# Attention, MoE and a second MoE layer on one core: every transpose of the attention on 128 rows, with an identity of exchanged halves

## The chip, the cores and the metric

The kernel runs on one core of a Trainium2 chip. The metric is the device time of one execution in microseconds (us). The engines are PE (TensorE: a matmul, and PEld, the load of its stationary operand), DVE (VectorE), ACT (ScalarE), POOL (GpSimd) and SP, which only issues transfers.

## What is computed

Two batches of twelve causal attention heads (448 positions, 64 wide) feed two feed-forward layers over 896 tokens. The reference, cut:

```python
scores = scale * np.matmul(q, k.transpose(0, 1, 3, 2))
scores = np.where(np.triu(np.ones((seq, seq), dtype=bool), k=1), -1e9, scores)
attn = np.exp(scores - scores.max(-1, keepdims=True))
x = np.matmul(attn / (attn.sum(-1, keepdims=True) + 1e-9), v)     # 2 x 12 heads
x = x.transpose(0, 2, 1, 3).reshape(896, 768)
x = ((1 / (1 + np.exp(-(x @ w_gate)))) * (x @ w_val)) @ w_out     # 768 -> 1536 -> 768
h = x @ w_in                                                      # 768 -> 1024
solu = h * softmax(h)
out = (solu - mean(solu)) / sqrt(var(solu) + 1e-6) * g_ln @ w_out2
```

## The kernel before, in words

Precision: each fp32 operand of a matmul is split into a high and a low part, and three of the four products are summed. The split of scores and values is done on POOL, ACT and DVE while the attention runs.

**Staging.** The attention (the first quarter of the time) is written as a software pipeline over `slots` = 96 steps: 24 heads with four blocks of queries each. In each step the order of each engine's work is written out by hand: first PE (`sc_mm`, the side step `rm`, the transposes `tr_mm`, a piece of `pv_mm`), then ACT, DVE, POOL. The table `SIDE` says in which step of a pair of heads (eight steps) each side task falls; `UNIT0` says it for the transposes. Then come the gate and value products (L594), the products with `w_out` (L621), the second layer's `h` (L651), its transposes (L694) and its output products (L712), all on PE.

**Blocks of queries.** The 448 queries of a head are cut as 64 + 128 + 128 + 128 (`QE`), but a block of scores always has 128 rows: in the first block the upper 64 rows are other data, and only rows 64 to 127 count. The keys are cut in 128s. So the block of the scores on the diagonal of key block j has its 64 useful rows in partitions 64 to 127; the queries of its partitions 0 to 63 come before these keys, and are masked.

**Transposes.** `tr_mm(h, u)` turns the exponentials `p` of head h, unit u, on PE: `p` is the stationary operand, a 128x128 identity `ident` the moving one, and the result goes to the PSUM tile `t`, which ACT (`tr_hi`) and DVE (`tr_lo`) split into `pt`. A full block takes 128 rows of `p` and moves 128 columns of `ident`. A half block takes partitions 64 to 127 alone and moves the 64x64 corner of `ident`. `sorted(blocks, ...)` puts the half blocks of a unit first. A unit with u = 1 has two half and three full blocks; one with u = 0 has one half and three full blocks for a head of even number, and two and three for an odd one (with the extra half block of the last keys, which `last_keys`, the step `lk`, has put there). `rs_mm(p)`, the step `rm`, does the same once for each pair of heads with the reciprocals of the sums, spread by POOL into `rx` (`rs_wide`, the step `rx`): one half block and three full ones.

**Names in the rows.** `s` is the scores' PSUM tile (4 buffers), `qks` the split queries and keys, `x` the values' product, `r` and `rb` the transposed reciprocals, `sum` and `rs` the sums and their reciprocals. L345 is `sc_mm`, L360 `sc_exp`, L354 `sc_max`, L383 `rs_mm`, L410 `tr_mm`, L417 `tr_hi`, L439 `pv_mm`, L241 the high part of q, L251 the low part of q, L365 `sums`, L369 `recips`, L446 `x_mul`. L230 is every subtraction and L220, L222, L224 every copy of the helpers, told apart by their tiles: POOL's L230 on `qks` is the low part of a key (`kl0`, `kl1`), POOL's L222 to `rx` is `rs_wide`, ACT's L220 to `qks` is the high part of the pair's second key (`kh1`), to which `kl1` must wait.

Of the kernel before, what the change touches and what calls it, by code (L numbers as in the profile page):

```python
# [10 lines left out]
F32 = mybir.dt.float32  # L11
# [8 lines left out]
B, H, S, D = 2, 12, 448, 64  # L20
# [4 lines left out]
QE = [64, 192, 320, 448]  # L25
POFF = [0, 128, 384, 768, 1280]
# [18 lines left out]
def attn_moe_moe2(ctx: ExitStack, tc: tile.TileContext, qk, v, w_gv, w_out, w_in2, w_out2, g_ln, out):  # L45
# [3 lines left out]
    nc = tc.nc  # L49
    ctx.enter_context(tc.manual_schedule())  # L50

    const = ctx.enter_context(tc.tile_pool(name="const", bufs=1))
# [4 lines left out]
    NGA = 1  # L57

    ident = const.tile([128, 128], F32, name="ident")
    identb = const.tile([128, 128], BF16, name="identb")  # L60
    maskb = const.tile([128, 128], BF16, name="maskb")
    g_sb = const.tile([128, NF2], F32, name="g_sb")
# [129 lines left out]
    with ExitStack() as actx:  # L192
# [89 lines left out]
        nc.vector.memset(warm, 0.0)  # L282
        nc.scalar.activation(out=warm, in_=warm, func=AF.Exp)
        make_identity(nc, ident)
        nc.vector.tensor_copy(out=identb, in_=ident)
        mask0 = one.tile([128, 128], F32, name="mask0")
        nc.gpsimd.memset(mask0, 0.0)
# [11 lines left out]
        p_t = [one.tile([128, POFF[NQ]], F32, name=f"p{i}") for i in range(NPB)]  # L299

        for i in range(NPB):
            for j in range(NQ - 1):
                nc.vector.memset(p_t[i][:, POFF[j] + QE[j]:POFF[j + 1]], 0.0)
        for i in range(2):
            for a in range(2):
                nc.scalar.copy(out=v2[i][:, a, :, D:2 * D], in_=zero.rearrange("p (j d) -> p j d", j=3))

        ps = ps_x.tile([128, S], F32, tag="x", name="warm")
# [69 lines left out]
        def rs_mm(p):  # L378
            ps = ps_rr[p] = ps_x.tile([128, S], F32, tag="x", name="r")
            rx = rx_t.pop(p).rearrange("p i a d -> p i (a d)")  # L380
            for i in range(NQ):
                lo = 0 if i else D
                nc.tensor.transpose(ps[:, QE[i] - 128 + lo:QE[i]], rx[lo:, i], ident[lo:, lo:])  # L383

        def rs_out(p):
            rb_t[p] = xfp.tile([128, S], F32, tag="rb", name="rb")
# [7 lines left out]
        def tr_width(h, u):  # L394
            return 512 if u or h % 2 else S

        def tr_mm(h, u):
            ps = ps_tr[h, u] = ps_t.tile([128, 512], F32, tag="t", name="t")
            pt = p_t[h % NPB]
            n, blocks = 0, []  # L400
            for j in UNITS[u]:
                for i in range(j, NQ):
                    lo = 64 if i == j else 0
                    blocks.append((lo, i, j, n))
                    n += 128 - lo
            if n < tr_width(h, u):
                blocks.append((64, 3, 3, n))

            for lo, i, j, n in sorted(blocks, key=lambda x: -x[0]):
                nc.tensor.transpose(ps[:, n:n + 128 - lo], pt[lo:, POFF[i] + j * 128:POFF[i] + (j + 1) * 128],  # L410
                                    ident[lo:, lo:])

        def tr_hi(h, u):
            if h not in pt_t:
# [45 lines left out]
        def early_tiles():  # L460
# [27 lines left out]
            vh=9, vl=11, xl=23, rr=12, lk=5)  # L488
        STEP = dict(
            sm=(sums, 'P'), rc=(recips, 'D'), rx=(rs_wide, ENG['rx']), rm=(rs_mm, 'E'), rr=(rs_out, ENG['rr']),  # L490
            xm=(x_mul, 'D'), xh=(x_hi, ENG['xh']), xl=(x_lo, ENG['xl']),
            vh=(prep_v_hi, ENG['vh']), vl=(prep_v_lo, ENG['vl']), lk=(last_keys, ENG['lk']),
# [27 lines left out]
        for s in range(slots + 32):  # L520
# [5 lines left out]
            if s >= 110 and left and next(early):  # L526
                left -= 1
            units(tr_mm, s)
            next(pv_now, None)

# [46 lines left out]
    with tc.tile_pool(name="psg", bufs=8, space=PSUM, reuse_waits="tile") as psg:  # L577
        for t in range(NF):
            bs = (1,) if t < NE else (0, 1)
            ps = {}  # L580
            ev = {}
            for i in range(2):
                c = 2 * t + i
# [23 lines left out]
    for m in range(NK):  # L607
        pm = php.tile([128, B, 512], F32, tag="h", name="pm")
        ps = [pm[:, b, :S] for b in range(B)]
        for i in range(2):  # L610
            c = 2 * NF + 2 * m + i
# [168 lines left out]
```

## Time and profile before

| | |
|---|---|
| time, median of 3 runs | 525.12 us (523.32 to 526.01) |
| profiled execution: its own time | 524.13 us |
| profiled execution: its span in the trace | 522.3 us |
| PE busy | 510.7 us, 98% of the span |
| DVE, POOL, ACT busy | 356.6 us (68%), 219.1 us (42%), 200.7 us (38%) |

The span runs from the first to the last recorded instruction; the own time of the same execution is 1.83 us longer. The shares are means over stages that differ: the attention occupies all four engines, the stages behind it mostly PE. The profile's PE time of one matmul includes its way through the array, so the spacing of two matmuls is read from their starts, not from their durations.

### The profile page before, as it was taken

What the parts mean: (1) busy time and instruction counts of PE and PEld (TensorE: products, weight loads), DVE (VectorE), ACT (ScalarE), POOL (GpSimd) and SP (SyncE); (2) the same over time, 40 slices, a digit from 0 to 9 for tenths busy, and PEclk for the clock granted to TensorE, in tenths of its full rate; (3) what the DMA queues carried; (4) which work ended last, traced back from release to release, by engine and by line L of the source; (5) the groups of instructions that cost most, each with busy time, mean ns of one, the idle gap of its engine ahead of it and who ended that gap; (6) DMA issues with size and microseconds to landing.
All of it is one profiled execution on the core that took longest, in us unless ns stands there. A gap on an engine that the chain in (4) does not pass through costs nothing. (4 is left out here: it accounts for less than half of the span.)

```text
span 522.3 us, 7577 instructions
## 1 busy us (share of the span) xinstructions
PE 510.7 (98%) x2786; PEld 458.1 (88%) x2786; DVE 356.6 (68%) x539; ACT 200.7 (38%) x446; POOL 219.1 (42%) x297
## 2 busy tenths in 40 slices
PE   6999999999999999999999999999999999999997
PEld 5888888888999998888988899999998888899997
DVE  5788888886566788778778766777782888741210
ACT  5678777784512323231332231212221434341211
POOL 4888999965313332322332331111142479720000
PEclk9999999999999999999999999999999999999999
DMA  7954645103333333443443333443431131000101
GB/s 200 286 141 118 155 111 137 49 20 118 125 122 90 125 110 111 149 162 127 155 131 122 130 122 100 162 153 132 158 122 60 61 122 62 0 31 30 61 31 60
DMA packets 15125, 58.30 MB, mean 112 GB/s; under 512 B 2160, under 2 KB 2672, under 8 KB 15088
## 3 DMA queue, kind: packets, MB, share of 16 engines
q1 hardware_dynamic: 15088, 57.81, 35.1%
q8 instruction: 22, 0.36, 0.3%
q14 instruction: 15, 0.12, 0.1%
HBM read 55.05 MB, written 2.75 MB: 111 GB/s over the span
## 5 line engine op out<-in xcount | busy, mean ns | idle before, releaser
L594 PE MATMUL gv<-xy,hl 128*128 128x448 f32 x828 | 170.5, 367 | 3.3 <-DVE hl L134 3.3
L594 PEld LDWEIGHTS gv<-xy,hl 128*128 128x128 f32 x828 | 154.5, 188 | 19.1 <-DVE hl L134 6.2
L621 PE MATMUL pm<-g,hl 128*128 128x448 f32 x432 | 87.7, 365 | 0.0
L621 PEld LDWEIGHTS pm<-g,hl 128*128 128x128 f32 x432 | 81.2, 188 | 6.4
L111 ACT ACTIVATE raw<-raw 128x768 f32<-128x768 f32 (+1 forms) x56 | 47.5, 858 | 56.4 <-DMA raw<-in_gv_dram 27.4
L114 DVE TENSOR_SCALAR t<-raw 128x768 int32<-128x768 int32 (+1 forms) x56 | 40.7, 726 | 34.8 <-ACT raw L111 33.5
L712 PE MATMUL po<-wo,lt 128*128 128x384 f32 x336 | 60.7, 340 | 0.0
L116 DVE SCALAR_TENSOR_TENSOR t<-raw,t 128x768 int32<-128x768 int32 (+1 forms) x56 | 59.4, 1060 | 1.9
L188 POOL TENSOR_TENSOR g<-wk,g 128x448 fp32r<-128x448 f32 x24 | 27.3, 1158 | 77.9 <-ACT g L187 77.9
L651 PE MATMUL h<-wi,xy 128*128 128x512 f32 x252 | 59.2, 395 | 0.0
L712 PEld LDWEIGHTS po<-wo,lt 128*128 128x128 f32 x336 | 58.7, 188 | 0.2 <-POOL wo L643 0.2
L651 PEld LDWEIGHTS h<-wi,xy 128*128 128x128 f32 x252 | 47.2, 187 | 11.4
L119 DVE SCALAR_TENSOR_TENSOR t<-raw,t 128x768 int32<-128x768 int32 (+1 forms) x56 | 53.5, 956 | 1.7
L130 POOL TENSOR_SCALAR hl<-t 128x768 fp32r<-128x768 f32 x36 | 34.3, 954 | 40.9 <-PE pm L621 29.9
L439 PE MATMUL x<-pt,v 128*128 128x448 f32 (+3 forms) x252 | 47.8, 323 | 0.0
L360 ACT ACTIVATE p<-s,sum 128x448 f32<-128x448 f32 (+1 forms) x96 | 46.2, 491 | 1.8 <-DVE sum L354 1.7
L345 PE MATMUL s<-qks 128*128 128x448 f32 (+1 forms) x192 | 43.8, 328 | 2.7 <-ACT p L360 1.6
L410 PE MATMUL t<-ident,p 128*128 128x128 f32 (+1 forms) x228 | 39.7, 284 | 0.0
L439 PEld LDWEIGHTS x<-pt,v 128*128 128x128 f32 x252 | 37.6, 190 | 0.7
L354 DVE TENSOR_REDUCE sum<-s 128x1 f32<-128x448 f32 (+1 forms) x96 | 36.7, 415 | 2.0 <-PE s L345 1.3
L134 DVE TENSOR_TENSOR hl<-t,hl 128x768 fp32r<-128x768 f32 x36 | 34.3, 952 | 3.8 <-POOL hl L130 3.7
L345 PEld LDWEIGHTS s<-qks 128*128 128x128 f32 x192 | 33.2, 209 | 3.9 <-POOL qks L230 2.1
(83 smaller groups left out, 539.8 us busy)
## 6 DMA issues: line engine op xcount, KB each, us to landing
raw<-in_gv_dram SPq DMA_DIRECT2D x24, 768.0 KB, 4.5
raw<-in_wo_dram SPq DMA_DIRECT2D x20, 768.0 KB, 4.3
qkr<-in_qk_dram SPq DMA_DIRECT2D x46, 224.0 KB, 3.9
raw<-in_wi_dram SPq DMA_DIRECT2D x12, 512.0 KB, 3.5
vr<-in_v_dram SPq DMA_DIRECT2D x12, 256.0 KB, 2.6
out_dram<-o SPq DMA_DIRECT2D x6, 384.0 KB, 2.3
qkr<-in_qk_dram SPq DMA_DIRECT2D x4, 112.0 KB, 2.6
out_dram<-o SPq DMA_DIRECT2D x2, 192.0 KB, 1.9
```

The costliest lines, as they stand in the source:

```text
L111: nc.scalar.activation(out=w1.bitcast(F32), in_=w1.bitcast(F32), func=AF.Copy, scale=2.0 ** -112)
L114: nc.vector.tensor_scalar(out=tt, in0=w1, scalar1=3, scalar2=None, op0=ALU.logical_shift_left)
L116: nc.vector.scalar_tensor_tensor(out=tt, in0=w1, scalar=-2 ** 31, in1=tt, op0=ALU.bitwise_and, op1=ALU.bitwise_or)
L119: nc.vector.scalar_tensor_tensor(out=tt, in0=w0, scalar=29, in1=tt, op0=ALU.logical_shift_right, op1=ALU.bitwise_or)
L345: nc.tensor.matmul(out=o, lhsT=l, rhs=r, start=(m == 0), stop=(m == 2))
L360: nc.scalar.activation(out=p_t[h % NPB][:, POFF[i]:POFF[i] + n], in_=ps_sc.pop(s), func=AF.Exp, bias=mx, scale=1.0, accum_out=sm)
L410: nc.tensor.transpose(ps[:, n:n + 128 - lo], pt[lo:, POFF[i] + j * 128:POFF[i] + (j + 1) * 128], ident[lo:, lo:])
L439: nc.tensor.matmul(out=ps[:, 128 * j:], lhsT=l, rhs=pt_t[h][:, c, u, c0:c0 + S - 128 * j], start=(n == 0), stop=(n == 20))
L594: nc.tensor.matmul(out=ps[i, b], lhsT=w[:, a, cs], rhs=xy[kk][:, x, b * S:(b + 1) * S], start=(kk == 0 and a == 0 and x == 0), stop=(kk == ...
L621: nc.tensor.matmul(out=ps[b], lhsT=w[:, a, cs], rhs=g_t[kk][:, x, b * S:(b + 1) * S], start=(kk == 0 and a == 0 and x == 0), stop=(kk == N ...
L651: nc.tensor.matmul(out=h[:, n * 512:(n + 1) * 512], lhsT=xy[kk][:, a, tk], rhs=wi[n * NK + kk][:, c], start=(kk == 0 and i == 0), stop=(kk ...
L712: nc.tensor.matmul(out=ps[n], lhsT=lts[k // 4][:, a, k % 4], rhs=wo[k][:, c, cs], start=(k == 0 and i == 0), stop=(k == NF2 - 1 and i == 2))
```

## The change

A second identity `identx` is made, whose column halves are exchanged. Every half block now takes all 128 rows of `p` (or `rx`) and moves 128 columns: its transposed 64 useful rows land where they did, and the transposed other 64 rows land beside them, in 64 columns of the same PSUM tile that a full block of the same unit writes afterwards. Where the half block stands at the start of its tile (or of the tile's first 64 columns), there are no columns to its left, so the useful half is turned to the left by `identx` and the other half lies to its right. The last 64 columns of `p` are set to zero once at the start, since the extra half block of a head of odd number now reads its other 64 rows there. The number and order of PE's transposes stay as they are: 228 in `tr_mm` and 48 in `rs_mm`, 84 and 12 of them half blocks. POOL has two copies more at the start, DVE three memsets.

```diff
@@ -57,6 +57,7 @@
     ident = const.tile([128, 128], F32, name="ident")
+    identx = const.tile([128, 128], F32, name="identx")
...
@@ -282,6 +283,9 @@
         make_identity(nc, ident)
+
+        nc.gpsimd.tensor_copy(out=identx[:, :D], in_=ident[:, D:])
+        nc.gpsimd.tensor_copy(out=identx[:, D:], in_=ident[:, :D])
         nc.vector.tensor_copy(out=identb, in_=ident)
...
@@ -301,6 +305,7 @@
             for j in range(NQ - 1):
                 nc.vector.memset(p_t[i][:, POFF[j] + QE[j]:POFF[j + 1]], 0.0)
+            nc.vector.memset(p_t[i][:, POFF[3] + QE[3]:], 0.0)
...
@@ -379,8 +384,8 @@
             for i in range(NQ):
-                lo = 0 if i else D
-                nc.tensor.transpose(ps[:, QE[i] - 128 + lo:QE[i]], rx[lo:, i], ident[lo:, lo:])
+
+                nc.tensor.transpose(ps[:, max(QE[i] - 128, 0):max(QE[i], 128)], rx[:, i], ident if i else identx)
...
@@ -407,8 +412,9 @@
             for lo, i, j, n in sorted(blocks, key=lambda x: -x[0]):
-                nc.tensor.transpose(ps[:, n:n + 128 - lo], pt[lo:, POFF[i] + j * 128:POFF[i] + (j + 1) * 128],
-                                    ident[lo:, lo:])
+                c = max(n - lo, 0)
+                nc.tensor.transpose(ps[:, c:c + 128], pt[:, POFF[i] + j * 128:POFF[i] + (j + 1) * 128],
+                                    identx if lo > n else ident)
```

## Rows read from the trace of the kernel before

**Rows 1.** Page, engines: busy us, share of the span, instructions.

```profile
PE 510.7 (98%) x2786; PEld 458.1 (88%) x2786; DVE 356.6 (68%) x539; ACT 200.7 (38%) x446; POOL 219.1 (42%) x297
```

**Rows 2.** A stretch of one pair: PE, PEld, DVE, ACT, POOL us (x), clock, DMA.

```profile
57.31:66.61 9.30, 9.30 (x70) 8.01 (x68) 8.05 (x19) 7.25 (x25) 8.52 (x13) 1.00 0.51 128
```

**Rows 3.** PEld, timeline about one unit: start us, us, line, shapes.

```profile
101.65 0.19 PEld L345 LDWEIGHTS s<-qks 128*128 128x128 f32 x1
101.97 0.14 PEld L410 LDWEIGHTS t<-ident,p 64*128 64x128 f32 x1
102.03 0.14 PEld L410 LDWEIGHTS t<-ident,p 64*128 64x128 f32 x1
102.24 0.14 PEld L410 LDWEIGHTS t<-ident,p 128*128 128x128 f32 x1
102.30 0.14 PEld L410 LDWEIGHTS t<-ident,p 128*128 128x128 f32 x1
102.41 0.14 PEld L410 LDWEIGHTS t<-ident,p 128*128 128x128 f32 x1
102.52 0.19 PEld L439 LDWEIGHTS x<-pt,v 128*128 128x128 f32 x1
```

**Rows 4.** PE, timeline: the scores' product just ahead of that unit.

```profile
101.80 0.25 PE L345 MATMUL s<-qks 128*128 128x192 f32 x1
```

**Rows 5.** Chain that ended last, a piece: start us, us, what, count.

```profile
463.95 0.87 PE tp L694 x8
464.82 8.44 PE po L712 x48
```

**Rows 6.** POOL, timeline of one pair; in brackets the idle time before, and its releaser.

```profile
69.36 1.43 POOL L230 TENSOR_TENSOR qks<-qkr,qks 64x448 fp32r<-64x448 f32 x1 [0.46 <-ACT qks L220]
...
72.97 0.91 POOL L222 TENSOR_SCALAR v<-vr 128x384 fp32r<-128x384 f32 x2
73.85 0.61 POOL L222 TENSOR_SCALAR rx<-rs 128x512 f32<-128x512 f32 x1
74.44 1.80 POOL L230 TENSOR_TENSOR v<-vr,v 128x384 fp32r<-128x384 f32 x2
```

**Rows 7.** PE, timeline: the reciprocals' transposes of that pair.

```profile
75.91 0.75 PE L383 MATMUL r<-ident,rx 64*128 64x64 f32 x4
```

**Rows 8.** POOL, timelines of an early and a late pair.

```profile
27.29 1.42 POOL L230 TENSOR_TENSOR v<-vr,v 128x384 fp32r<-128x384 f32 x2
...
29.90 1.14 POOL L230 TENSOR_TENSOR qks<-qkr,qks 64x448 fp32r<-64x448 f32 x1
32.16 1.44 POOL L230 TENSOR_TENSOR qks<-qkr,qks 64x448 fp32r<-64x448 f32 x1 [1.13 <-ACT qks L220]
...
109.64 0.78 POOL L222 TENSOR_SCALAR v<-vr 128x384 fp32r<-128x384 f32 x2
```

**Rows 9.** DVE, timeline of the pair of rows 6.

```profile
69.17 0.62 DVE L251 SCALAR_TENSOR_TENSOR qks<-qkr,qks 128x448 fp32r<-128x448 f32 x1
...
72.93 0.20 DVE L369 RECIPROCAL rs<-rs 128x8 f32<-128x8 f32 x1 [0.33 <-POOL rs L365]
73.05 0.68 DVE L224 CAST qks<-qkr 128x448 fp32r<-128x448 f32 x1
...
74.91 1.00 DVE L251 SCALAR_TENSOR_TENSOR qks<-qkr,qks 128x448 fp32r<-128x448 f32 x1
```

**Rows 10.** Timeline of the start.

```profile
2.24 0.70 DVE L303 MEMSET p<- 128x64 f32 x9
...
4.75 0.62 DVE L230 TENSOR_TENSOR qks<-qkr,qks 64x448 fp32r<-64x448 f32 x1 [1.80 <-ACT qks L220]
5.46 0.57 POOL L241 TENSOR_SCALAR qks<-qkr 128x448 fp32r<-128x448 f32 x1 [3.65 <-DMA qkr<-in_qk_dram]
...
12.70 0.24 POOL L222 TENSOR_SCALAR p<-p 64x64 f32<-64x64 f32 x1
```

**Rows 11.** PE, timeline: the last pair's reciprocals.

```profile
121.11 0.75 PE L383 MATMUL r<-ident,rx 64*128 64x64 f32 x4 [0.61 <-POOL rx L222]
```

## The prediction

> **What bounds the kernel now.** I read the page first: PE is busy 98% of the span [rows 1]. That is a mean, so I read the attention, the only stage that the change touches, by stretches. Eight steps of the pipeline, one pair of heads, take 9.30 us, and PE is busy in all of them, while POOL has 8.52, DVE 8.05 and ACT 7.25 us of work [rows 2]. The period repeats: the reciprocals' transposes of the seventh pair start at 75.91 [rows 7], and every earlier or later pair's lie a multiple of 9.30 away (the second at 29.41, the tenth at 103.81), but for the first and the last. So PE sets the pace, with POOL only 8% behind. The timelines then show what the others wait for: POOL stands still once in a pair, 0.46 us, until ACT has made the second key's high part [rows 6], and that copy comes behind PE's transposes in ACT's order. POOL is thus pulled along by PE and not against its own end. Its `rx` is done at 73.85 + 0.61 = 74.46, 1.45 us ahead of the transposes that read it [rows 6, 7].
>
> **What a half block costs on PE.** The starts of the loads about one unit give it [rows 3]. The product ahead of the unit starts at 101.80 [rows 4] and has 192 columns. Columns cost 8.44 us / 48 / 384 = 0.46 ns each in the output products [rows 5], so it streams until 101.89. The first half block's load starts only at 101.97: 0.08 us of pause, and then 0.06 us of load that nothing covers (the next load follows at 102.03). Entry: 0.14 us. The step from the last half block to the first full one is 0.21 us (102.03 to 102.24) where two full blocks lie 0.11 apart (102.30 to 102.41). Exit: 0.10 us. A half block behind a half block costs only 0.06 us, so where there are two, one is 0.05 us cheaper than a full one.
>
> Full height throughout has a row too: eight transposes of `e`, all on 128 rows, take 0.87 us between two runs of output products, 0.109 us each, and the products ahead and behind show no gap [rows 5]. So a load of 128 rows hides behind the stream ahead of it. I take 0.11 us for a half block on 128 rows, entry and exit gone. The bounds: 0.06 us (as now), and 0.17 us (0.06 load and 0.11 stream one after the other).
>
> The Trainium skill, page "TensorE: Matmul & The Clock Gate", Part 3, "What overlaps and what doesn't", says that weight loads overlap with running matmuls only when their row groups differ. That speaks against this change, since blocks of equal height share all row groups; by it the pauses at the entry would stay, which is the second rival's time below. The 0.87 us of rows 5 don't agree with it.
>
> **Per pair.** Five groups: the reciprocals (one half block), one unit with one half block, three with two. Two groups follow a 64-column product, whose 0.03 us of stream hides only half of the load, so they win 0.11 at the entry; three win 0.14. Sum: 3 x 0.14 + 2 x 0.11 + 5 x 0.10 - 3 x 0.05 = 0.99 us, so 1.0 of 9.30. The reciprocals and the unit right behind them are 0.4 of it. The order of the instructions and what waits for what stay.
>
> **What POOL lets through.** PE alone would come down to 8.3 us a pair. POOL without its wait needs 9.30 - 0.46 = 8.84. So POOL falls behind PE until its lead at `rx` is used up, and then PE waits for `rx`. The longest way to the tenth pair's reciprocals at 103.81 begins on PE, changes to POOL at the last long wait (1.13 us, ending at 32.16 [rows 8]), and stays there:
> - until 32.16 at PE's pace: one pair 1.0, the second pair's reciprocals and unit 0.4, the units before the first pair's reciprocals 0.2 (between 0 and 0.6, three units of 0.2; PE still waits for its first operands there): 1.6 us;
> - seven waits of POOL, one per pair from 41.46 to 97.26, at 0.46: 3.2 us;
> - POOL's lead of 1.45 us, of which I leave 0.1 for the hand-over and 0.25 because DVE, which already waits 0.33 for POOL's sums [rows 9], passes a later POOL on to the maxima, to ACT's exponentials and so to the score buffers: 1.1 us.
>
> Behind it POOL has no next keys and values to split, so the pair up to the eleventh counts at PE's pace, 1.0, and the eleventh's reciprocals and unit 0.4. The last pair's I count at nothing: its reciprocals already wait 0.61 us for POOL's `rx` [rows 11], a chain from the last scores over maxima, exponentials and sums that no transposes shorten. Sum 7.3 us. The stages behind move up as they are; their weight chunks are prepared in steps of the same pipeline.
>
> POOL's durations are the unsure part. Three of its operations are longer where DVE's L251 or L224 runs beside them: `kl1` 1.43 against 1.14 for `kl0`, the values' low parts 1.80 against 1.42, their high parts 0.91 against 0.78 [rows 6, 8], beside DVE's operations of 0.62, 1.00 and 0.68 us [rows 9]. That is 0.80 us a pair. As POOL slides against DVE these may be missed (8.0 us a pair, below PE's 8.3) or grow; I keep 0.80, since a POOL without pauses meets all three.
>
> **The start.** Two POOL copies cost at most what a 64x64 one does at 12.70, 0.24 each, and three DVE memsets 0.70 / 9 = 0.08 each [rows 10]. POOL then idles 3.65 us for the first transfer and DVE 1.80 [rows 10], so both are hidden; uncovered they would be 0.5 us.
>
> **The forecast.** The sum stands against the profiled execution: 524.13 - 7.3 = 516.8. That execution lies 0.99 below the median of the three runs, and nothing says which is typical, so I start midway, at 524.6: **517.3 us**. Within 0.5% (2.6 us) a measurement can hardly tell a change: the three runs span 2.7.
>
> **Rivals.**
> - PE keeps the pace: POOL's collisions fall apart and it needs under 8.3. Then 12 x 1.0 less 0.4 at the end: 11.6 us, 513.0. For it: 8.04 without collisions. Against: POOL would have no pause left in which to miss DVE.
> - The entry pause stays: it belongs to the change from scores to transposes, not to the height. Rows 5 show loads hidden behind 384 columns, here 64 or 192 stream ahead. Then 0.99 - 0.64 = 0.35 a pair, 4.2 us, 520.4.
> - POOL's floor is 9.30 after all, what it saves in waiting going into longer collisions: 1.6 and the lead, 2.6 us in all, 522.0. That would be a change that does what it says on PE and hardly shows.
> - Slower: POOL stops for the whole of each of DVE's three operations, 0.62 + 0.62 + 0.68 = 1.92 us instead of 0.80, and needs 8.04 + 1.92 = 9.96 a pair. Over nine pairs that is 5.9 us more than now: 530.5. It decides from 1.26 us of collisions a pair, where 9.30 is reached. Against it: `kl1` now loses 0.29 beside a DVE operation of 0.62.
>
> The page "SBUF — State Buffer" of the Trainium skill, "Who interferes with whom", has this as a rule: whoever issues first holds the port pair of DVE and GpSimd for its whole instruction, and the other is blocked fully. Rows 6 and 8 show about half of that.
>
> **Chances.** Forecast 0.52, PE keeps the pace 0.20, entry pause 0.12, POOL's floor at 9.30 0.10, slower 0.06. The range 512.5 to 521.5 holds the first three with the bounds of the block's cost (at 0.17 us PE saves 1.0 - 8 x 0.06 = 0.5 a pair, 6.2 us, 518.4) and leaves out the slower case, most of the fourth and the rim of the second. Faster by over 0.5%: 0.88 (half of the fourth is in it, roughly), within: 0.06, slower: 0.06.
>
> **What will show it.** Right on PE: the loads of a unit 0.11 apart, the first right after the start of the product ahead, and no step of 0.21. Right on POOL: the bracketed wait of 0.46 gone, POOL's share of a pair near 97%, a new wait of PE for `rx`, the period near 8.85. A period of 8.3 with POOL pauses is the first rival; loads 0.17 late at each unit's start, the second; POOL's operations longer than in rows 6, the last two. What would make it all wrong is a wait that I have not seen: PE's scores on ACT's exponentials, or transposes on DVE's low parts, with most of the 1.0 us in it.

## The result, and the profile after

The changed kernel takes 517.68 us, the median of 4 runs (516.69 to 518.95); the kernel before takes 525.57 us in 4 runs beside them (523.32 to 527.0). The ratio is 0.986, with an interval of [0.9822, 0.9898], so it is faster by 7.9 us. A second series later gave 518.33 us in 6 runs against 524.88 in 23, a ratio of 0.9869 [0.9831, 0.9906], or 6.6 us. The forecast was 517.3.

The profiled execution took 518.95 us, its span is 517.2. The page's row of engines, in the columns of [rows 1], shows that PE lost 8.0 us of busy time and that its share fell by a point:

```profile
PE 502.7 (97%) x2786; PEld 455.7 (88%) x2786; DVE 360.9 (70%) x542; ACT 200.3 (39%) x446; POOL 220.0 (43%) x299
```

Two stretches of one pair of heads, in the columns of [rows 2]:

```profile
43.47:52.36 8.89, 8.84 (x73) 8.00 (x71) 8.21 (x18) 7.25 (x24) 8.57 (x13) 1.00 0.50 134
52.36:61.26 8.90, 8.83 (x72) 7.99 (x70) 8.22 (x18) 7.23 (x24) 8.58 (x13) 1.00 0.50 137
```

A pair now takes 8.89 us instead of 9.30, seven times in a row. POOL's work is nearly what it was (8.57; 8.52 before), but now fills 96% of the pair (it was 92%). PE is still marked busy for 8.84 of it, and that is misleading: the same instructions of PE fit in 8.35 once POOL has less to do (the run with `vh='A'` below).

The loads about one unit, on PEld, answer to [rows 3]:

```profile
73.06 0.30 PEld L350 LDWEIGHTS s<-qks 128*128 128x128 f32 x2
73.32 0.14 PEld L416 LDWEIGHTS t<-identx,p 128*128 128x128 f32 x1
73.40 0.36 PEld L416 LDWEIGHTS t<-ident,p 128*128 128x128 f32 x3
73.73 0.45 PEld L445 LDWEIGHTS x<-pt,v 128*128 128x128 f32 x3
```

From the first block's load at 73.32 to the load of the values' product at 73.73 the four blocks take 0.41, 0.10 each. The first load starts just when the product ahead, 192 columns long, starts in the trace (73.31), where before it started 0.08 after these columns had streamed; the step of 0.21 behind the half blocks is gone too.

POOL's timeline, one pair and the start of the next, which answers to [rows 6], and behind it PE's transposes of the reciprocals that the last of these rows feeds, which answer to [rows 7]:

```profile
60.22 0.90 POOL L223 TENSOR_SCALAR v<-vr 128x384 fp32r<-128x384 f32 x2
61.09 0.61 POOL L223 TENSOR_SCALAR rx<-rs 128x512 f32<-128x512 f32 x1
61.67 1.80 POOL L231 TENSOR_TENSOR v<-vr,v 128x384 fp32r<-128x384 f32 x2
63.45 0.56 POOL L242 TENSOR_SCALAR qks<-qkr 128x448 fp32r<-128x448 f32 x1
64.09 0.24 POOL L223 TENSOR_SCALAR p<-p 64x64 f32<-64x64 f32 x1
64.29 2.63 POOL L231 TENSOR_TENSOR qks<-qkr,qks 64x448 fp32r<-64x448 f32 x2
67.01 1.15 POOL L231 TENSOR_TENSOR xy<-xf,xy 128x448 fp32r<-128x448 f32 x1
68.12 0.56 POOL L242 TENSOR_SCALAR qks<-qkr 128x448 fp32r<-128x448 f32 x1
68.77 0.25 POOL L370 TENSOR_SCALAR rs<-sum 128x8 f32<-128x8 f32 x1
69.10 0.91 POOL L223 TENSOR_SCALAR v<-vr 128x384 fp32r<-128x384 f32 x2
69.97 0.61 POOL L223 TENSOR_SCALAR rx<-rs 128x512 f32<-128x512 f32 x1
```

```profile
70.64 0.33 PE L388 MATMUL r<-identx,rx 128*128 128x128 f32 x1
```

No row of POOL has a bracket, where [rows 6] has one of 0.46: POOL waits for nobody. Its `rx` ends at 69.97 + 0.61 = 70.58 and PE's transposes begin 0.06 later; before they followed 1.45 behind. PE's wait stands in the view of waits for 43 to 97 us (engine, tile, line, releaser: us in all, count, the longest), and so does what else waits for POOL:

```profile
ACT p L365 <- DVE sum L359: 9.1, 12, 0.8
DVE rs L374 <- POOL rs L370: 4.1, 6, 0.7
PEld r L388 <- POOL rx L223: 1.3, 6, 0.2
```

By the means, DVE waits 0.7 for POOL's sums in each of the six pairs (0.33 in [rows 9]), ACT's exponentials 0.8 for DVE's maxima twice a pair, PE's load 0.2 for `rx`. So POOL holds back DVE and PE directly. ACT's wait, which the same view of before doesn't have, is for DVE; that it goes back to POOL is read from this order and not tested by itself.

### The profile page after: what moved, and what is told of

Same layout as the page of the kernel before. It is cut to its first block, busy times and chain, and to the rows that moved or that the text cites. A ratio compares the mean times of both kernels' runs of the same rounds, so it can differ in the third digit from the quotient of the medians.

```text
span 517.2 us, 7582 instructions
## 1 busy us (share of the span) xinstructions
PE 502.7 (97%) x2786; PEld 455.7 (88%) x2786; DVE 360.9 (70%) x542; ACT 200.3 (39%) x446; POOL 220.0 (43%) x299
## 5 line engine op out<-in xcount | busy, mean ns | idle before, releaser
L627 PE MATMUL pm<-g,hl 128*128 128x448 f32 x432 | 89.4, 368 | 0.0
L112 ACT ACTIVATE raw<-raw 128x768 f32<-128x768 f32 (+1 forms) x56 | 47.4, 857 | 55.0 <-DMA raw<-in_wo_dram 26.7
L117 DVE SCALAR_TENSOR_TENSOR t<-raw,t 128x768 int32<-128x768 int32 (+1 forms) x56 | 59.4, 1061 | 1.9
L120 DVE SCALAR_TENSOR_TENSOR t<-raw,t 128x768 int32<-128x768 int32 (+1 forms) x56 | 54.9, 980 | 1.7
L131 POOL TENSOR_SCALAR wi<-t 128x512 fp32r<-128x512 f32 x12 | 7.4, 618 | 66.3 <-DVE t L120 66.3
```

The costliest lines, as they stand in the source:

```text
L112: nc.scalar.activation(out=w1.bitcast(F32), in_=w1.bitcast(F32), func=AF.Copy, scale=2.0 ** -112)
L117: nc.vector.scalar_tensor_tensor(out=tt, in0=w1, scalar=-2 ** 31, in1=tt, op0=ALU.bitwise_and, op1=ALU.bitwise_or)
L120: nc.vector.scalar_tensor_tensor(out=tt, in0=w0, scalar=29, in1=tt, op0=ALU.logical_shift_right, op1=ALU.bitwise_or)
L131: nc.gpsimd.tensor_scalar(out=hi, in0=t_t[it], scalar1=g, scalar2=1.0, op0=ALU.mult, op1=ALU.mult)
L627: nc.tensor.matmul(out=ps[b], lhsT=w[:, a, cs], rhs=g_t[kk][:, x, b * S:(b + 1) * S], start=(kk == 0 and a == 0 and x == 0), stop=(kk == N ...
```

## The experiments

**One extra copy on POOL.** Is POOL really slack before and the bound after? The same scratch copy, as large as `rx`, in each pair of both kernels:

```diff
+        dz = [one.tile([128, 512], F32, name=f"dz{i}") for i in range(2)]
+        nc.vector.memset(dz[0], 0.0)
...
-            vh=9, vl=11, xl=23, rr=12, lk=5)
+            vh=9, vl=11, xl=23, rr=12, lk=5, ds=13)
...
-            ... lk=(last_keys, ENG['lk']),
+            ... lk=(last_keys, ENG['lk']), ds=(lambda p: on('P', dz[1], dz[0]), 'P'),
```

> The kernel before with one more POOL copy per pair (128x512, 0.61 us by rows 6's rx, on a scratch tile that nobody reads). Theory P (PE sets the pace before, POOL only after the change): POOL's wait of 0.46 us and its lead of 1.45 us at rx take the copy up, so between 0 and +1.5 us against the kernel before. Rival Q (POOL's queue already sets the pace before): +0.61 x 10 pairs = about +6 us.

The kernel before with the copy: 528.15 us in 10 runs, a ratio of 1.0064 [1.0031, 1.0097], so 3.4 us by the ratio. The windows of a pair early and one late:

```profile
48.06:57.36 9.30, 9.30 (x70) 8.01 (x69) 8.28 (x18) 7.10 (x24) 8.81 (x13) 1.00 0.47 128
76.20:85.80 9.60, 9.55 (x70) 8.09 (x69) 7.88 (x18) 7.44 (x23) 9.11 (x14) 1.00 0.50 126
```

For the first five pairs nothing happens: POOL uses up its lead. Then the pairs take 9.60. So POOL did have slack, and the lead goes first, as read; the rival, by which the copy is paid for in every pair, falls. The size is a miss: 3.4 us, where 0 to 1.5 was expected. In the profiled execution the last reciprocals come 1.4 us later than in that of before (122.52 and 121.11), which is within those bounds; but that execution took 525.72 us, 2.4 less than the median of its series, so the rest of the difference stays open.

> The changed kernel with the same extra POOL copy per pair. Theory P: its pairs of 8.89 us are POOL's own, so they become 9.5 us and eight or nine of them cost +4.9 to +5.5 us against the changed kernel. Rival R (the 8.89 us are PE's own cost of the blocks of 128 rows, or DVE's): the copy goes into slack, less than +1.5 us.

The changed kernel with the copy: 524.25 us, 0.997 [0.9943, 0.9996] of the kernel before, so 6.6 us above the first series of the changed one. One of its pairs:

```profile
46.60:56.17 9.57, 8.82 (x68) 8.03 (x69) 7.89 (x18) 7.35 (x23) 9.09 (x14) 1.00 0.50 125
```

9.57 is 8.89 + 0.68: from the third pair on each pays the copy in full, and POOL is the bound after the change. The 6.6 us are above the 4.9 to 5.5 that were expected. In the profiles the last reciprocals come 6.7 us later than in the changed kernel (121.48 and 114.80): 4.8 are these seven pairs, and 1.9 a first pair that ends later (20.48 and 18.55), of which more below.

**Work taken from POOL.** The values' high part goes from POOL to ACT, in both kernels:

```diff
-        ENG = dict(... vh='P', ...)
+        ENG = dict(... vh='A', ...)
```

> The kernel before with the values' high parts (two POOL copies, 0.91 us a pair) made by ACT, which has 7.24 us of work in 9.30. Theory P: PE keeps 9.30 us a pair, so within 1 us of the kernel before. Rival Q: up to 5 us faster.

> The changed kernel with the values' high parts made by ACT. Theory P: POOL falls to about 8.0 us a pair, and PE's own 8.3 us (or DVE's 8.2 of work) becomes the bound: pairs of 8.3 to 8.5 us, 3 to 5 us faster than the changed kernel, near 513 to 515 us. Rival R: pairs stay at 8.89 us and the time stays within 1 us. A third case: ACT, with 7.24 + 0.9 us of work in order, becomes late itself, and the time grows.

Before: 525.79 us, 1.0009 [0.9977, 1.004], pairs of 9.30. Relief of POOL gives nothing where PE is the bound. After: 514.49 us in 4 runs, 0.9788 [0.9745, 0.9832], the lowest median here. A pair of the first and one of the second, and one operation of the second's POOL:

```profile
58.40:67.70 9.30, 9.30 (x70) 8.01 (x68) 7.54 (x18) 7.95 (x27) 7.74 (x11) 1.00 0.46 128
44.01:52.36 8.35, 8.35 (x71) 8.00 (x69) 7.40 (x19) 7.86 (x26) 7.52 (x11) 1.00 0.56 143
```

```profile
63.34 1.24 POOL L231 TENSOR_TENSOR qks<-qkr,qks 64x448 fp32r<-64x448 f32 x1 [0.26 <-ACT qks L221]
```

POOL waits for ACT again (0.26), and PE sets the pace at 8.35. So the change is worth 0.95 us a pair on PE, and POOL lets 0.41 of it through.

**What a half block costs on PE.** The parts of the change, each where PE is the bound. First the reciprocals alone (the `tr_mm` hunk undone), then the units alone (the `rs_mm` hunk undone, with `vh='A'`):

> Only the reciprocals' half block on 128 rows; the scores' transposes as before. By the terms (entry 0.11, exit 0.10) PE's pair falls by 0.21 to 9.09 us, which is above POOL's 8.84 to 8.89, so PE keeps the pace: 11 or 12 pairs, 2.3 to 2.5 us faster than the kernel before. If POOL already were the bound, nothing.

> The scores' transposes alone on 128 rows, the reciprocals' half block as before, and the values' high parts on ACT so that POOL does not hide the difference. By the terms 0.21 us a pair more than the run with all blocks on 128 rows and the same relief (8.35): 8.56 us a pair, about 2.4 us slower than that run's 514.5, near 517.

The first gave 522.68 us, 0.9949 [0.9918, 0.9981], the second 514.94 us, 0.9805 [0.976, 0.985]. A pair of each:

```profile
48.70:57.80 9.10, 9.10 (x70) 7.98 (x69) 8.05 (x18) 7.23 (x24) 8.50 (x13) 1.00 0.52 131
```

```profile
44.88:53.43 8.55, 8.55 (x70) 8.03 (x68) 7.39 (x18) 7.85 (x27) 7.52 (x11) 1.00 0.57 140
```

The reciprocals' half block is worth 9.30 - 9.10 = 0.20 and, from the other side, 8.55 - 8.35 = 0.20; the working had 0.21. In time the second is a miss: near 517 was expected, 2.4 above the 514.49, and the medians lie 0.45 apart, with intervals that overlap. The profiled executions do show it: the last reciprocals come at 112.73 and at 110.37.

Then the rival that a pause belongs to the change from scores to transposes and not to the height, which is the number of rows. In the kernel with `vh='A'` the second half block of each unit with two goes back to 64 rows, so that the height changes in the middle of the transposes:

```diff
+                if lo and n:
+                    nc.tensor.transpose(ps[:, n:n + 64], pt[lo:, ...], ident[lo:, lo:])
+                    continue
```

> As the run with the relief on ACT, but in a unit with two half blocks the second one is on 64 rows again, so that it stands between blocks of 128 rows of its own kind. If the pause belongs to the step from one height to another (my reading): the entry 0.14 now comes inside the unit, exit 0.10 behind it, less 0.05 for the shorter block, 0.19 us for each of three units: 8.92 us a pair, 5 to 6 us slower than 514.5, near 520. If it belongs to the step from the scores' products to the transposes (the second rival of the prediction): only the exit, 8.35 + 3 x 0.05 = 8.5 us a pair, near 516.

It took 520.63 us, 0.9909 [0.9882, 0.9935]. Its pair, and its loads about a unit:

```profile
46.86:55.89 9.03, 9.03 (x71) 8.08 (x69) 7.49 (x18) 7.84 (x26) 7.75 (x11) 1.00 0.51 132
```

```profile
62.79 0.19 PEld L350 LDWEIGHTS s<-qks 128*128 128x128 f32 x1
62.95 0.14 PEld L419 LDWEIGHTS t<-identx,p 128*128 128x128 f32 x1
63.23 0.14 PEld L416 LDWEIGHTS t<-ident,p 64*128 64x128 f32 x1
63.43 0.14 PEld L419 LDWEIGHTS t<-ident,p 128*128 128x128 f32 x1
```

A pair is 0.68 longer than 8.35, 0.23 for each of three units, although a 64-row block streams fewer columns. The steps are 0.28 into the 64 rows and 0.20 out of them, where two full blocks lie 0.11 apart [rows 3]. Between transposes the kind of work does not change, only the height and with it the number of columns; columns alone change without a pause above, where a product of 192 stands ahead of a transpose of 128. So the pauses are the height's. The height's reading had 8.92 and the rival 8.5: the sign is settled, the size is a little above.

The Trainium skill, page "TensorEngine Tiling (Array Packing)", section "Key Properties", says that a change of the tiling mode makes the engine drain first. If blocks on 64 rows are such a mode, the steps of 0.28 and 0.20 agree with that.

**The start.** The first reciprocals of the changed kernel came 1.9 us earlier than before, where 0.2 was expected, and the clock's record differs there. So the change in the first pair alone, in all pairs but the first, a second series of the changed kernel, and one more profiled run of each of the two kernels. The edit against the changed kernel, cut; the second form has `p >= 1` and `h >= 2`:

```diff
+                if p < 1:
+                    nc.tensor.transpose(... rx[:, i], ident if i else identx)
+                else:
+                    lo = 0 if i else D
+                    nc.tensor.transpose(... rx[lo:, i], ident[lo:, lo:])
...
+                if not (h < 2):
+                    nc.tensor.transpose(... pt[lo:, ...], ident[lo:, lo:])
+                    continue
```

> Only the first pair of heads (and its reciprocals) on 128 rows, the other eleven pairs as before, so that PE keeps 9.30 us a pair and what the start gains stays in the time. So far the fast clock was granted for good between 15.7 and 18.0 us in four of five profiles with every transposed block of the first pair on 128 rows or one unit's half block short of it (20.3 in the fifth), and between 19.9 and 22.7 us in four profiles with the scores' transposes as before. Theory D (the change brings the rise earlier): rise before 18.1 us, first reciprocals before 20 us, 2 to 3 us faster than the kernel before. Theory C (chance): rise anywhere from 15 to 23 us, and the time within 1.2 us of the kernel before (the pair's own 0.99 us at most).

> The other eleven pairs on 128 rows, the first pair as before. Theory D: rise after 19.8 us, first reciprocals near 20.5 us, 1 to 2 us slower than the changed kernel's 518, since POOL then starts its own run later. Theory C: no difference to the changed kernel beyond 1 us.

> The changed kernel as it is, for a second profile and more times. Its first profile had the fast clock from 15.65 us, the kernel before only from about 19.9. Theory C (when the clock rises is chance, and POOL, not PE, sets the end of the attention): with a late rise the first reciprocals start near 20.5 as before, the pairs still come to 8.89 us, and the time stays 516 to 519 us. Rival D (the change itself brings the earlier rise, and 2 us of the gain are from it): the rise is near 15.7 again.

> The kernel before once more, for one more start. Theory D: fast clock for good after 19.8 us. Theory C: anywhere from 15 to 23 us.

> The changed kernel once more, for one more start. Theory D: fast clock for good before 18.1 us. Theory C: anywhere from 15 to 23 us. Pairs of 8.89 us in either case.

The first pair alone gives 523.29 us against 524.83, 0.9966 [0.9947, 0.9986]: 1.8 us by the ratio, of one pair in twelve. Theory D (the change brings the rise forward) expected 2 to 3, theory C (chance) at most 1.2, and the interval, 0.7 to 2.8 us, holds parts of both. All but the first give 520.0 us, 0.9889 [0.9849, 0.9929], an interval that overlaps the changed kernel's, so this run alone doesn't separate them. The second series and the second profiled run of the changed kernel (518.33 and 516.84 us) repeat the first, and the second profiled run of the kernel before took 522.82.

These two profiled runs have traces that hold a record of the clock from the start. The kernel before, and then the changed kernel, the stretch at the lower clock and one behind it:

```profile
7.90:18.00 10.10, 7.68 (x35) 6.23 (x33) 7.22 (x18) 6.28 (x21) 8.27 (x12) 0.50 1.05 249
18.20:25.00 6.80, 6.80 (x52) 5.72 (x51) 6.51 (x13) 5.73 (x21) 5.54 (x9) 1.00 1.04 342
```

```profile
8.70:15.40 6.70, 5.01 (x21) 4.31 (x22) 5.03 (x13) 4.96 (x18) 5.25 (x7) 0.50 1.02 262
15.50:20.00 4.50, 4.35 (x36) 3.95 (x35) 4.35 (x10) 3.49 (x13) 4.34 (x8) 1.00 1.04 244
```

The last column but two is the granted clock: 0.50 is 1.2 GHz, 1.00 is 2.4 GHz. PE is busy for about three quarters of the low stretch in both (76% and 75%), and yet the clock rises at 18.10 in the one and at 15.43 in the other. Theory D wanted the first of these after 19.8, so it has a miss there, too. Over all traces of this study, the rise for good lies between 15.43 and 17.98 in seven of the eight in which blocks of the first pair's units take 128 rows, wholly or in part; in the eighth, the changed kernel with the extra copy on POOL, it lies at 20.34. In the six with these units as before it lies between 18.10 and 26.67. So the two groups are apart but for one trace, which speaks for theory D and doesn't prove it. What an earlier rise does: in the first executions profiled, the scores with 320 columns behind the second unit of transposes run at 16.16 in the changed kernel, at the higher clock, while in the kernel before they come at 16.92, at the lower (0.78 instead of 0.48 us for two products):

```profile
16.16 0.48 PE L350 MATMUL s<-qks 128*128 128x320 f32 x2
```

```profile
16.92 0.78 PE L345 MATMUL s<-qks 128*128 128x320 f32 x2
```

In the kernel with all but the first pair changed, where the clock rises at 26.67, products with 320 columns still take 0.78 at 25.04:

```profile
25.04 0.78 PE L350 MATMUL s<-qks 128*128 128x320 f32 x2
```

## Why the forecast was right, point by point

**PE's saving: right.** 0.99 a pair was the sum, 0.95 is measured (9.30 to 8.35), its part for the reciprocals 0.21 and 0.20. The load of 128 rows hides behind the stream ahead, as read from the transposes of `e` [rows 5]. The rule of the Trainium skill that spoke against it, page "TensorE: Matmul & The Clock Gate", Part 3, "What overlaps and what doesn't" (loads overlap with running matmuls only where row groups differ), does not agree with these loads: neighbours share all row groups, and a load of 0.14 us has its successor 0.10 behind it.

**POOL as the next bound: right.** The floor was worked out as 8.84; the pairs take 8.89. The collisions that were to stay at 0.80 a pair grew by 0.09: the second key's lower part takes 1.52 in the trace (1.43 in [rows 6]), while the values' parts, 0.90 and 1.80, are as they were. The wait of 0.46 went, the new wait is PE's for `rx`, and the copy on POOL and its relief say the same by experiment.

**The lead and the seven waits: somewhat too large.** From the first to the tenth reciprocals the working had 1.4 + 3.2 + 1.1 = 5.7 us. The profile of before has 103.81 - 20.46 = 83.35 and the one of after 97.32 - 18.55 = 78.77, so 4.6: 2.9 in seven pairs at 0.41 (3.2 expected), and 1.7 in the first two, where PE's pace and POOL's lead were to give 2.5.

**The start: wrong by more than that, and the cause was not foreseen.** 0.2 was expected and 1.9 measured (1.4 if two traces of before and three of after are averaged). The two additions at the start are hidden, as expected: POOL's copies are over at 1.82, and then POOL still idles 3.10 us for the first transfer, as DVE does 1.07 us behind its memsets:

```profile
1.59 0.23 POOL L288 COPY identx<-ident 128x64 f32<-128x64 f32 x1
3.56 0.11 DVE L308 MEMSET p<- 128x64 f32 x1
4.74 0.62 DVE L231 TENSOR_TENSOR qks<-qkr,qks 64x448 fp32r<-64x448 f32 x1 [1.07 <-ACT qks L221]
5.42 0.56 POOL L242 TENSOR_SCALAR qks<-qkr 128x448 fp32r<-128x448 f32 x1 [3.10 <-DMA qkr<-in_qk_dram]
```

What the working missed is PE's clock, which is low in most of the first pair. Every price was read from stretches at the higher clock, and no step said when it rises. In the kernel with the first pair alone the first reciprocals stand at 18.72, and it gains 1.8 us, that pair's own saving on PE (about 1) included. That an earlier rise saves time is in the products' times; that the change brings the rise forward, rather than chance, is likely and not proven.

**The eleventh pair: the term that failed.** It was counted at PE's pace, 1.0 up to its reciprocals and 0.4 behind them, since POOL has less to do there. The pair up to the eleventh reciprocals gave 0.2 (9.09 instead of 9.30), and the stretch from there to the last ones lost 0.4 (8.39 instead of 8.00) where it was to gain 0.4. The windows of these two pairs, of before and then of after:

```profile
103.81:113.11 9.30, 9.30 (x70) 8.01 (x68) 7.69 (x18) 8.03 (x26) 8.24 (x13) 1.00 0.11 28
113.11:121.11 8.00, 7.39 (x52) 6.19 (x50) 7.18 (x14) 5.55 (x18) 4.17 (x7) 1.00 0.30 98
```

```profile
97.32:106.41 9.09, 8.93 (x69) 8.04 (x69) 8.91 (x19) 8.06 (x25) 8.76 (x12) 1.00 0.11 31
106.41:114.80 8.39, 6.62 (x52) 6.15 (x51) 8.19 (x15) 5.82 (x18) 5.20 (x10) 1.00 0.28 94
```

The third engine is DVE: 98% busy in both of these pairs, where it had 83% and 90%. Some of its operations take longer. In DVE's timeline, before and after, the lower part of q and the first step of a weight chunk:

```profile
106.37 0.62 DVE L251 SCALAR_TENSOR_TENSOR qks<-qkr,qks 128x448 fp32r<-128x448 f32 x1
111.97 0.84 DVE L114 TENSOR_SCALAR t<-raw 128x768 int32<-128x768 int32 x1
```

```profile
100.43 1.06 DVE L252 SCALAR_TENSOR_TENSOR qks<-qkr,qks 128x448 fp32r<-128x448 f32 x1
105.55 1.35 DVE L115 TENSOR_SCALAR t<-raw 128x768 int32<-128x768 int32 x1
```

Together they are 0.95 longer, and POOL runs lower parts beside both (2.64 us from 99.86, 1.75 from 105.47). I had looked for collisions in POOL's durations only; DVE, which has its own share of them, was counted as idle enough. Its maxima then hold ACT's exponentials and POOL's sums, and the last reciprocals wait 1.00 for `rx` where they waited 0.61 [rows 11]:

```profile
114.80 0.33 PE L388 MATMUL r<-identx,rx 128*128 128x128 f32 x1 [1.00 <-POOL rx L223]
```

That DVE is the bound of these two pairs is read from the rows. One run on record bears on it, the changed kernel with `vh='A'`, the windows of whose last two pairs are:

```profile
94.10:102.94 8.84, 8.61 (x70) 8.02 (x69) 7.33 (x18) 8.35 (x27) 7.54 (x11) 1.00 0.11 32
102.94:110.37 7.43, 6.62 (x53) 6.14 (x51) 7.22 (x14) 6.23 (x20) 3.40 (x5) 1.00 0.35 106
```

There the same two operations of DVE take 0.62 (at 96.34) and 0.56 (at 102.08), DVE is busy for 7.33 of 8.84 and 7.22 of 7.43, and the two pairs take 16.27 instead of 17.48. So with work taken from POOL DVE's long operations are gone and 1.2 us come back, which fits the collisions as the cause; but that edit loads ACT as well, and no run changed these two operations alone.

**The sum.** By the tenth reciprocals 5.9 us was forecast and 6.5 measured, by the last ones 7.3 and 6.3. With the averages over two traces of before and three of after these are 6.0 and 5.8. Three errors thus cancel in part. In the first executions profiled the earlier clock, which wasn't foreseen, gave 1.7 too much before the first reciprocals; the lead and the waits gave 1.1 too little, and the last two pairs, which don't follow PE, 1.6 too little. That the forecast and the measured median lie 0.4 us apart is therefore partly luck; the pace of the pairs, 8.84 and 8.89, is not. Behind the attention nothing changes but by chance: the products with `w_out` took 89.28 us in this execution and in that of the kernel with the first pair alone, and 87.55 or 87.56 in the twelve other traces, two of the changed kernel among them.

That the medians differ by 6.6 to 7.9 us and the traces by less has a likely reason in the clock again. Of the 61 runs of the kernel before in the three later series, 25 have a record that shows a low clock at the start. In 17 of these the mean granted clock is 0.983 or 0.984, in 8 it is 0.989 to 0.993, and the medians are 526.07 and 523.04 us. In the 15 such runs of kernels in which the first pair's units are wholly on 128 rows it is 0.989 to 0.993 each time. So the longer stretch at the low clock, 3.0 us dearer by these medians, is the common one before, and the 15 don't show it; the two traces of before on which I average are those with the earliest rise (18.10 and 19.93) of the six. This is argued from the runs' clocks; no run holds the clock fixed.

**The rivals.** PE keeps the pace (513.0): it would need POOL's collisions to fall apart, and they didn't; with POOL relieved the time is 514.49. The entry pause stays (520.4): no such pause is in the loads, and the mixed heights show that it belongs to the height. POOL's floor at 9.30 (522.0) and POOL blocked for whole operations (530.5): pairs of 8.89 with 8.57 of work rule out both. (The third rival's own sum is off: 1.6 and a lead of 1.1 make 2.7, and it leaves out, without a reason given, the 1.4 us of the eleventh pair that the forecast counts; with both it would have been 520.5.)

## What to carry to other kernels

A transpose on 64 rows among neighbours on 128 costs PE about 0.2 us each time (0.20 for the reciprocals, 0.23 in the mixed units); filling the array with rows whose results land where something else is written afterwards removes that. When the engine that sets the pace gets faster, work out what the next engine needs without its waits, and do so for every stretch with its own mix of work, with the third engine too: here POOL let 0.41 of 0.95 us through, and DVE in the last pairs less. Then the next step is to give that engine's work away: the same move that gave nothing before the change (1.0009) brought the changed kernel to 514.49 us.

## What the runs showed of the hardware, unexpected

The granted clock of PE rises from 1.2 to 2.4 GHz earlier with 128-row blocks in the first pair's units (15.4 to 18.0 us, but for one trace at 20.3) than without (18.1 to 26.7), although PE is busy for three quarters of the low stretch in both of the traces shown. Why stays open: the two forms differ in rows, in columns and in pauses at once, no run separates these, and the one late trace shows that the form of the blocks is not all of it.

Operations of DVE and POOL that overlap stretch each other: a POOL operation of 1.14 us takes up to 1.44 [rows 8], a DVE operation of 0.62 up to 1.06. Which of the two pays is not fixed: for the second key's lower part and q's lower part beside it, POOL alone pays before (1.43 and 0.62 [rows 6, 9]) and both pay after (1.52 and 1.05 in the pairs that POOL sets). So a price has to be looked for in both engines' rows.
